# Keys and values of a token tile from one pass over weights that lie side by side, in a linear-attention and MLP kernel

## The chip, the cores and the metric

The kernel runs on one core of a Trainium2 chip. The metric is the device time of one execution, in microseconds (us). Of the kernel before, three runs are given; their median is the time that the change is compared with.

## The reference

Input x has 2048 tokens of D = 640 columns, everything in float32. After a layernorm without weights, xn feeds two branches, and their product is added to x:

```python
xn = _layernorm(x, axis=-1)
q, k, v = (xn @ wqkv) split by thirds, H = 32 heads of Dh = 20
pq = einsum("bhsd,hdf->bhsf", q, w_phi);  pk = einsum("bhsd,hdf->bhsf", k, w_phi)
phi_q = concat([softmax(pq), softmax(-pq)]);  phi_k = concat([softmax(pk), softmax(-pk)])
kv = einsum("bhsf,bhsd->bhfd", phi_k, v);  z = phi_k summed over the tokens
o = (phi_q kv) / (phi_q z + 1e-6);  s = o @ wo
g = silu(gelu(xn @ w1 + b1) @ w2 + b2)
result = x + s * g
```

The hidden width of the second branch is 1536. The change touches only the first part of the first branch: k and v, the features of k, and what they wait for.

## The kernel before, in words

**Arithmetic.** A float32 matrix product is made of products of a reduced type (fp32r in the profile). Each operand is split into an upper part (the value rounded to the type) and a lower part (value minus upper part). `PASSES` lists the three of the four combinations that are computed: upper with upper, upper with lower, lower with upper. The 640 rows of a weight are KC = 5 slices of 128, so one projection of a tile of 128 tokens takes 5 x 3 = 15 steps, and each step has two products (`MATMUL` rows of the profile) of 320 columns, one for each of two PSUM banks.

**Tiles and their order.** The 2048 tokens are 16 tiles of 128 rows. Two tiles make a pair; tile t is half o = t % 2 of pair q = t // 2. The transposed, split x of the pairs stands in `xp` and `beside` (`b` or `b12` in the profile); `stat_x` (L256) picks the 128 x 128 block that a product loads as its stationary operand. Tiles 0 to 7 are loaded as rows (`x_in`, L455), normalised in place and transposed on TensorE (`transpose_x`, L312; its copies out of PSUM are `plain`, L252 on ACT and L254 on DVE). For tiles 8 to 15 the transposed x is loaded from memory instead, and only the statistics are computed from rows: `pair_stats` (L286) runs the statistics on DVE (L197), and for the second tile of a pair it stores mean and factor to memory (L293) and loads them back into all partitions as `bc` (L295). Both are issued by SP, whose instructions run in order, so that a load issued behind L295 goes out only after L295 did.

**Weights.** The weights of queries and keys are multiplied by w_phi ahead of time: `fold` (L168) makes one slice with six small products (L173) into PSUM; `fold_w` (L178) takes its upper part on ACT (L183) and its lower part on DVE (L184). The five slices of the keys, `wk_s`, are made at the start, those of the queries, `wq_s`, between the tiles: slice 0 in tile 3, slice 1 in tile 4, slices 2 and 3 in tile 5, slice 4 in tile 6. The values' weights `wv_s` are loaded and split (`split_w`, L144: upper on ACT, lower on POOL or DVE). Each slice of each weight is one buffer of 2 x 640 columns, upper and lower part.

**PSUM.** `bankA()` hands out one of three buffers of two banks each in turn; `bankB()` hands out one of two single banks, and one of those is held by the accumulators `kv` through the whole stage. The chip's PSUM has no other bank left.

**One tile.** `project(t, ws)` (L323, products at L332) fills a bankA buffer with 30 products of 320 columns. For the keys, `feat1` (L341) reads it on DVE: maximum, minimum (L345, L346), the subtraction (L349), and their difference; then POOL makes the second half (L353). `feat2` (L357) is the exponential on ACT. `key_fin` (L389) sums on DVE, and POOL scales (L371). `value(t)` (L374) is a projection of its own, whose bank ACT copies out (L380) into rows of 21 columns a head. `kv_acc` (L395) multiplies key features and values into `kv` with 32 small products (L403). `query(t)` (L383) projects with `wq_s` and sends the features to memory.

**Order.** In this stage the order of every engine is that of the program text (`manual_schedule`, L462 and L468); each engine works through its instructions in order, and only semaphores between engines make it wait. Tiles 0 and 1 are written out (L499 to L520); a loop runs tiles 2 to 5 (L521 to L541) and another tiles 6 to 15 (L543 to L589). In the first loop the order of a tile is: key projection, `kv_acc` of tile t - 2, key features, in tile 5 the fold of query slice 2, the statistics, then the value projection with the transposes of tile t + 2 in its midst, the exponential, the fold of a query slice, and `key_fin`. Tile 6 has the key projection, `kv_acc` of tile 4, the load of tile 11, statistics of tile 10, features, the fold of query slice 4, value projection, `key_fin`, the first two queries. From tile 7 on, each tile has one or two queries. At the end of tile 15 the first weights of the MLP are brought into their forms (`w1_forms`, L412, with L426 on ACT and L427 on POOL), and the MLP follows in units (products at L650 and L679), with the numerators (L780), the denominators and the output projection (L844) among them.

Of the kernel before, what the change touches and what calls it, by code (L numbers as in the profile page):

```python
# [20 lines left out]
KC = D // P  # L21
HALF = D // 2
# [4 lines left out]
VW = 704  # L27
LN_EPS = 1e-5
DEN_EPS = 1e-6
NH = 2  # L30
SLOTS = 4
FOLD_W = 800
# [14 lines left out]
def hedgehog_gated_mlp_kernel(ctx: ExitStack, tc: tile.TileContext, x, xt_in, wqk, bd, wv, wo, w1, b1, w2, b2, out_t):  # L47
    nc = tc.nc
# [32 lines left out]
    def slab(dt, name, shape=(P, 2, D)):  # L81
        return slabs.tile(list(shape), dt, tag="S", name=name)
# [95 lines left out]
    def fold_w(tl, cs, name, dst):  # L178
        for c in cs:
            ps, mm = fold(tl, c)  # L180
            sl = slab(F32R, f"{name}{c}")
            s3 = sl[:].rearrange("p s (a b) -> p s a b", a=2)
            nc.scalar.activation(s3[:, 0], ps[:, :, :HALF], AF.Copy)  # L183
            lo = nc.vector.tensor_tensor(s3[:, 1], ps[:, :, :HALF], s3[:, 0].bitcast(F32), op=OP.subtract)  # L184
            dst.append(sl)
        return mm, lo


# [123 lines left out]
    def transpose_x(t):  # L312
        q, o = divmod(t, 2)
        xn = xns.pop(t)
        ps = bankA()
        flat = ps[:].rearrange("p a b -> p (a b)")
        for k in range(KC):
            nc.tensor.transpose(flat[:, k * P:(k + 1) * P], xn[:, k * P:(k + 1) * P], ident[:])  # L318
        plain(q, o, flat[:, :D].rearrange("p (k t) -> p k t", t=P))

    PASSES = ((0, 0), (0, 1), (1, 0))

    def project(t, ws, mid=None, at_k=3):  # L323
        q, o = divmod(t, 2)
        ps = bankA()
        n = 0
        for k in range(KC):
            if k == at_k and mid is not None:
                mid()
            for a, b in PASSES:  # L330
                for hf in range(2):
                    nc.tensor.matmul(ps[:, hf, :HALF], stat_x(q, o, k, a),  # L332
                                     ws[k][:, b, hf * HALF:(hf + 1) * HALF],
                                     start=n == 0, stop=n == 3 * KC - 1)
                n += 1
        return ps

    def heads(ps):
        return ps[:, :, :HALF].rearrange("p a (h d) -> p a h d", d=DH)

    def feat1(ps):  # L341
        p4 = heads(ps)
        mx = small.tile([P, 2, 16], F32, tag="mx", name="mx")
        mn = small.tile([P, 2, 16], F32, tag="mn", name="mn")
        nc.vector.tensor_reduce(mx[:], p4, axis=AX.X, op=OP.max)  # L345
        nc.vector.tensor_reduce(mn[:], p4, axis=AX.X, op=OP.min)  # L346
        e = slab(F32, "e")[:]
        e5 = e.rearrange("p a (h s d) -> p a h s d", s=2, d=DH)
        nc.vector.tensor_tensor(e5[:, :, :, 0, :], p4, mx[:, :, :, None].to_broadcast([P, 2, 16, DH]),  # L349
                                op=OP.subtract)  # L350
        nr = small.tile([P, 2, 16], F32, tag="nr", name="nr")
        last_feat[0] = nc.vector.tensor_tensor(nr[:], mn[:], mx[:], op=OP.subtract)  # L352
        nc.gpsimd.tensor_tensor(e5[:, :, :, 1, :], nr[:, :, :, None].to_broadcast([P, 2, 16, DH]),  # L353
                                e5[:, :, :, 0, :], op=OP.subtract)
        return e.rearrange("p a b -> p (a b)")
# [5 lines left out]
    def features(ps):  # L361
        return feat2(feat1(ps))
# [9 lines left out]


    def value(t, mid=None):  # L374
        ps = project(t, wv_s, mid)
        v = row([P, VW], F32, "v")
        v3 = v[:, :32 * (DH + 1)].rearrange("p (h d) -> p h d", d=DH + 1)
        nc.gpsimd.memset(v3[:, :, DH:DH + 1], 1.0)
        nc.gpsimd.memset(v[:, 32 * (DH + 1):], 0.0)
        nc.scalar.activation(v3[:, :, :DH].rearrange("p (a h) d -> p a h d", a=2), heads(ps), AF.Copy)  # L380
        return v

    def query(t):  # L383
        ef = features(project(t, wq_s))
        nc.scalar.dma_start(e_dram[_tok(t)], ef)

    kvp = [None]
# [16 lines left out]
                                         phi[:, 40 * h:40 * h + 40], start=t == 0 and s == 0, stop=t == NT - 1,  # L404
                                         skip_group_check=True)

    vs, es, phis, xns, wk_s, wq_s = {}, {}, {}, {}, [], []

    def load_w1(g):
        return [load_raw(w1[f]) for f in range(g * GF, (g + 1) * GF)]  # L410
# [67 lines left out]
    x_in(7)  # L478
    nc.sync.dma_start(b1t[:], b1)
    nc.sync.dma_start(b2t[:], b2)  # L480
    wv_s = []

    def split_v(c):
        wv_s.append(split_w(wv_raw[c][:], "wv", "dve" if c == 3 else "pool"))

    nc.vector.tensor_tensor(foldb[:120, :, :120].rearrange("p i (k d) -> p i k d", k=6),
                            foldc[:120, :, None, :].to_broadcast([120, 6, 6, DH]),
                            hmask[:120, None, :, None].to_broadcast([120, 6, 6, DH]), op=OP.mult)
    fold_w(wkT, range(1), "wk", wk_s)
    norm_a(0)  # L490
    fold_w(wkT, range(1, 2), "wk", wk_s)
    norm_b(0)
    fold_w(wkT, range(2, 4), "wk", wk_s)
    transpose_x(0)
    norm_a(1)
    fold_w(wkT, range(4, KC), "wk", wk_s)
    norm_act(1)
    norm_a(2)
    split_v(0)  # L499
    kvp[0] = bankB("kv")  # L500
    pk = project(0, wk_s, lambda: transpose_x(1), 4)
    norm_act(2)
    split_v(1)
    split_v(2)
    es[0] = feat1(pk)
    split_v(3)
    pk = project(1, wk_s, lambda: transpose_x(2))
    x_in(8)
    x_in(9)
    load_xr(4)  # L510
# [8 lines left out]
    norm(4)  # L519
    phis[1] = key_fin(es.pop(1))  # L520
    for t in range(2, 6):  # L521
        pk = project(t, wk_s)
        kv_acc(t - 2, phis.pop(t - 2), vs.pop(t - 2))
        es[t] = feat1(pk)
        if t == 5:
            fold_w(wqT, range(2, 3), "wq", wq_s)
        if t < 4:
            norm(t + 3)
        if t == 3:
            norm(7)  # L530
        if t > 3:
            pair_stats(t + 4)
        if t in (3, 4):
            spill(t - 3)
        if t == 5:
            x_in(10)
        vs[t] = value(t, (lambda: transpose_x(t + 2)) if t < 6 else None)
        feat2(es[t])
        if t >= 3:
            fold_w(wqT, range(t - 3 + (t > 4), t - 2 + (t > 4)), "wq", wq_s)  # L540
        phis[t] = key_fin(es.pop(t))  # L541
    queries = iter(range(NT))
    for t in range(6, NT):  # L543
        u = t + 4
        pk = project(t, wk_s)
        if t == 6:
            kv_acc(4, phis.pop(4), vs.pop(4))
        if u < NT:
            if u + 1 < NT:
                x_in(u + 1)  # L550
            pair_stats(u)
            if u % 2:
                load_xr(u // 2)
        if t in (6, 8):
            spill(t // 2 - 1)
        if t % 2 == 0 and 6 < t < NT - 2:
            pair_sub((t + 2) // 2)
        es[t] = feat1(pk)
        if t == 6:
            pair_sub(4)  # L560
            fold_w(wqT, range(4, KC), "wq", wq_s)
        if t % 2 == 0 and t < NT - 2:
            pair_mul((t + 2) // 2)
        if t == 12:
            w1r = load_w1(0)
        if t % 2 and t < NT - 2:
            t_sums((t + 1) // 2)
        vs[t] = value(t)
        feat2(es[t])
        phis[t] = key_fin(es.pop(t))  # L570
        if t % 2 == 0 and 6 < t < NT - 2:
            pair_plain((t + 2) // 2)
        if t % 2 and t < NT - 2:
            t_split((t + 1) // 2)
        if t == 6:
            query(next(queries))
            query(next(queries))
            pair_plain(4)
        if t == NT - 1:
            w1f = w1_forms(w1r)  # L580
            next(w1f)
            next(w1f)
        if t >= 7:
            query(next(queries))
        kv_acc(t - 1, phis.pop(t - 1), vs.pop(t - 1))
        if t == NT - 1:
            next(w1f)
        if 7 <= t < 10:
            query(next(queries))  # L589
    t = NT - 1  # L590
    w2r = [load_raw(w2[f * P:(f + 1) * P, :]) for f in range(GF)]
    pq = project(next(queries), wq_s)
    e_14 = feat1(pq)
    next(w1f)
    w1g = next(w1f)
# [263 lines left out]
        return [load_raw(w2[f * P:(f + 1) * P, :]) for f in range(g * GF, (g + 1) * GF)]  # L859

    kvr = kv_rest()
    e_last = feat1(project(next(queries), wq_s))
    startup.close()
    phase1.close()
    early_psum.close()
# [223 lines left out]
```

## Time and profile before

| | us |
|---|---|
| runs of the kernel before | 682.97, 684.15, 684.3 |
| median | 684.15 |
| span of the profiled execution (first to last instruction) | 681.1 |
| device time of the profiled execution | not given by its page |
| TensorE (PE) | 676.4 busy, 99%, 4727 products |
| weight loads (PEld, beside PE) | 592.0, 87% |
| VectorE (DVE) | 454.8, 67%, 729 instructions |
| GpSimd (POOL) | 382.2, 56%, 351 |
| ScalarE (ACT) | 253.0, 37%, 400 |

Busy shares are means over the span. The granted clock of TensorE is at nine tenths or more in each of the 40 slices of the page. In the rows that follow, a line of the timeline has the start in us from the beginning of the span, the length in us, the engine, the line of the kernel, the operation, output and input with their shapes, the count of instructions that are taken together (x30), and in brackets the engine's idle time in front and what ended it. A line of the chain has the time, the length, the engine, the output and line, and the count. SPq is SP's queue of DMA issues.

### The profile page before, as it was taken

The numbers are of one execution on the slowest core, as the hardware profiler recorded it, in microseconds if no ns is written. First come the engines' busy times: TensorE is split into PE (matmuls) and PEld (weight loads), VectorE is DVE, ScalarE is ACT, GpSimd is POOL, SyncE is SP. The second block draws the span as 40 slices with busy tenths as digits, with TensorE's granted clock in tenths as the row PEclk, the third lists the DMA queues.
The fourth block names the chain that finished last, engine by engine and source line by source line (L and its number), as shares of the span: only waits on it lengthen the run. The fifth ranks groups of instructions, "written<-read, shape, count | busy, mean of one in ns | idle before, by whom it ended". The sixth has DMA issues, their size and how long they took to land.

```text
span 681.1 us, 11991 instructions
## 1 busy us (share of the span) xinstructions
PE 676.4 (99%) x4727; PEld 592.0 (87%) x4727; DVE 454.8 (67%) x729; ACT 253.0 (37%) x400; POOL 382.2 (56%) x351
## 2 busy tenths in 40 slices
PE   9999999999999999999999999999999999999998
PEld 9999999999999998888888888888888887777876
DVE  5786665887876466586978784576876655774232
ACT  3523214333223337144254247533133254425440
POOL 3653254757767375857978952726446640783221
PEclk9999999999999999999999999999999999999999
DMA  8820144633451333329688696476363491888423
GB/s 330 311 80 1 11 142 100 227 93 137 69 200 60 115 138 135 117 88 348 209 273 278 237 426 280 129 259 224 139 216 137 151 398 47 321 296 291 150 94 109
DMA packets 73966, 125.42 MB, mean 184 GB/s; under 512 B 5822, under 2 KB 42686, under 8 KB 73014
## 3 DMA queue, kind: packets, MB, share of 16 engines
q1 hardware_dynamic: 71606, 114.17, 49.3%
q10 hardware_dynamic: 2304, 10.49, 4.4%
q8 instruction: 37, 0.61, 0.4%
q14 instruction: 19, 0.16, 0.1%
HBM read 79.54 MB, written 45.10 MB: 183 GB/s over the span
## 4 chain that ended last, share of the span: by engine, by line
PE 96%; DVE 1%; POOL 1%; issue 1%; ACT 0%; POOLq 0%
PE pA L332 30%; PE pB L679 24%; PE pB L650 22%; PE pB L844 11%; PE pB L780 3%; PE pB L769 2%; PE kv L403 2%; PE pA L173 1%; POOL wv L148 1%; PE pA L466 1%; PE pA L318 1%; PE pB L787 1%; DVE st L197 0%; DVE wk L184 0%; PE pB L624 0%
## 5 line engine op out<-in xcount | busy, mean ns | idle before, releaser
L679 PE MATMUL pB<-hs,w2s 128*128 128x512 f32 x720 | 167.1, 390 | 0.0
L679 PEld LDWEIGHTS pB<-hs,w2s 128*128 128x128 f32 x720 | 134.6, 188 | 29.4 <-PE pB L780 0.8
L650 PE MATMUL pB<-xp,w1s 128*128 128x512 f32 x324 | 81.4, 390 | 0.0
L650 PE MATMUL pB<-xd,w1s 128*128 128x512 f32 x324 | 79.3, 389 | 0.0
L358 ACT ACTIVATE e<-e 128x1280 f32<-128x1280 f32 x32 | 40.7, 1272 | 90.1 <-POOL e L353 89.5
L844 PE MATMUL pB<-oT,wo 128*128 128x512 f32 (+2 forms) x315 | 73.9, 386 | 0.0
L688 DVE TENSOR_TENSOR y<-pB,y 128x512 f32<-128x512 f32 x100 | 63.9, 680 | 12.4 <-PE pB L679 12.2
L650 PEld LDWEIGHTS pB<-xp,w1s 128*128 128x128 f32 x324 | 60.7, 188 | 12.9 <-DVE pB L925 0.4
L650 PEld LDWEIGHTS pB<-xd,w1s 128*128 128x128 f32 x324 | 60.8, 188 | 12.6
L844 PEld LDWEIGHTS pB<-oT,wo 128*128 128x128 f32 x315 | 57.1, 188 | 14.2 <-ACT ph L772 1.2
L371 POOL TENSOR_TENSOR e<-e,rc 128x1280 f32<-128x1280 f32 x16 | 39.0, 2438 | 48.8 <-DVE rc L391 48.4
L371 POOL TENSOR_TENSOR eq<-eq,rc 128x1280 f32<-128x1280 f32 x16 | 37.9, 2369 | 50.2 <-DVE rc L738 50.2
L353 POOL TENSOR_TENSOR e<-nr,e 128x640 f32<-128x640 f32 x32 | 45.5, 1424 | 30.1 <-DVE nr L352 27.7
L332 PE MATMUL pA<-wv,xp 128*128 128x320 f32 x384 | 60.7, 311 | 0.3 <-POOL wv L148 0.3
L655 ACT ACTIVATE pB<-pB,b1t 128x512 f32<-128x512 f32 x48 | 31.8, 662 | 77.2 <-DVE pB L925 27.6
L332 PE MATMUL pA<-wk,xp 128*128 128x320 f32 x384 | 59.9, 311 | 0.0
L332 PE MATMUL pA<-wq,xp 128*128 128x320 f32 x384 | 59.0, 309 | 0.0
L332 PEld LDWEIGHTS pA<-wv,xp 128*128 128x128 f32 x384 | 56.9, 188 | 0.6 <-POOL wv L148 0.5
L332 PEld LDWEIGHTS pA<-wq,xp 128*128 128x128 f32 x384 | 56.9, 188 | 0.1
L332 PEld LDWEIGHTS pA<-wk,xp 128*128 128x128 f32 x384 | 56.8, 188 | 0.1
L725 POOL TENSOR_TENSOR ez<-eq,zrep 128x1280 f32<-128x1280 f32 x16 | 47.3, 2959 | 0.2 <-PE pB L780 0.2
L427 POOL TENSOR_TENSOR w1s<-raw,w1s 128x640 fp32r<-128x640 f32 (+1 forms) x18 | 25.7, 1428 | 36.4 <-ACT w1s L426 29.2
(145 smaller groups left out, 1053.3 us busy)
## 6 DMA issues: line engine op xcount, KB each, us to landing
raw<-in_w_dram SPq DMA_DIRECT2D x42, 320.0 KB, 4.7
e_dram<-e ACTq DMA_DIRECT2D x16, 640.0 KB, 3.8
eq<-e_dram SPq DMA_DIRECT2D x16, 640.0 KB, 6.6
phi_dram<-eq SPq DMA_DIRECT2D x16, 640.0 KB, 3.5
phi<-phi_dram SPq DMA_DIRECT2D x16, 640.0 KB, 9.0
xt<-in_x_dram SPq DMA_DIRECT2D x16, 320.0 KB, 5.7
xres<-in_xt_dram SPq DMA_DIRECT2D x20, 256.0 KB, 4.3
out_dram<-xres SPq DMA_DIRECT2D x18, 256.0 KB, 3.0
```

What stands on the lines that cost most here:

```text
L332: nc.tensor.matmul(ps[:, hf, :HALF], stat_x(q, o, k, a), ws[k][:, b, hf * HALF:(hf + 1) * HALF], start=n == 0, stop=n == 3 * KC - 1)
L353: nc.gpsimd.tensor_tensor(e5[:, :, :, 1, :], nr[:, :, :, None].to_broadcast([P, 2, 16, DH]), e5[:, :, :, 0, :], op=OP.subtract)
L358: nc.scalar.activation(ef, ef, AF.Exp)
L371: nc.gpsimd.tensor_tensor(e3, e3, rc[:, :, None].to_broadcast([P, 64, DH]), op=OP.mult)
L427: nc.gpsimd.tensor_tensor(sl[:, 1, :n], src, sl[:, 0, :n].bitcast(F32), op=OP.subtract)
L650: nc.tensor.matmul(bank[ch][:], tl[:, a, off + wo_:off + wo_ + P], mov(blk, b), start=new and n == 0, stop=n == len(mms) - 1, skip_group_c ...
L655: nc.scalar.activation(ps, ps, AF.Gelu_apprx_tanh, bias=b1t[:, f:f + 1])
L679: nc.tensor.matmul(ps[:], ws[i][:, b, d * P:(d + 1) * P], hs[o][i][:, a, :], start=i == n == 0, stop=(i, n) == (GF - 1, 2), skip_group_che ...
L688: nc.vector.tensor_tensor(y, ps[:], y, op=OP.add)
L725: nc.gpsimd.tensor_tensor(zv, ef, zf, op=OP.mult)
L780: nc.tensor.matmul(po[64 * e:64 * e + 64, :256], bdk[:n, 2 * j + e, :], ph[:n, e * 256:(e + 1) * 256], start=True, stop=True)
L844: nc.tensor.matmul(ps[:, mv], w, o[:, mv], start=n == 0, stop=n == 15, skip_group_check=True)
```

## The change

**Weights.** `wkv` replaces `wk_s` and `wv_s`. For each of the five slices it holds two buffers, one of upper and one of lower parts, and each has 640 columns of keys and, right behind them, 640 of values. `fold_w` writes the key half and `split_v` the value half; their work is the same as before. The number of buffers and their size stay as they were.

**Projection.** For tiles 2 to 15 a new `project_kv` takes the place of the two calls of `project`. The 1280 columns are cut at 512 and at KV1 = 1020. A first pass has 15 steps of two products, columns 0 to 511 and 512 to 1019, into the two banks of one bankA buffer, laid out flat: all 640 key columns and the first 19 heads of the values. A second pass has 15 products of 260 columns, the last 13 heads of the values, into the free bank of bankB. The transposes of tile t + 2, in tiles 2 to 5, stand between the passes. So a tile has 45 products where it had 60, for the same 15 x 1280 columns.

**Readers.** `keys_of` gives the key features the first 640 columns of the flat buffer; they reach 128 columns into the second bank, where the values begin. `values_of` gives the values in two pieces, and `value_row` copies each with an ACT instruction of its own: 19 heads from the second bank of bankA and 13 from bankB.

**Order.** Both passes now stand at the head of a tile, ahead of `kv_acc` in the text, and the value copies stand directly behind the key features: ahead of the fold of query slice 2 in tile 5 and of slice 4 in tile 6, and ahead of the statistics in tiles 2 to 5. Tiles 0 and 1 and all queries keep `project`, with the weight given as a function (`w_part`).

```diff
+KV1 = 1020
...
-            sl = slab(F32R, f"{name}{c}")
-            s3 = sl[:].rearrange("p s (a b) -> p s a b", a=2)
-            nc.scalar.activation(s3[:, 0], ps[:, :, :HALF], AF.Copy)
-            lo = nc.vector.tensor_tensor(s3[:, 1], ps[:, :, :HALF], s3[:, 0].bitcast(F32), op=OP.subtract)
-            dst.append(sl)
+            if dst is wkv:
+                dst.append([slab(F32R, f"{name}{c}{b}") for b in "hl"])
+                s0, s1 = (w[:, 0, :].rearrange("p (a b) -> p a b", a=2) for w in dst[c])
+            else:
+                sl = slab(F32R, f"{name}{c}")
+                s0, s1 = (sl[:, b, :].rearrange("p (a b) -> p a b", a=2) for b in range(2))
+                dst.append(sl)
+            nc.scalar.activation(s0, ps[:, :, :HALF], AF.Copy)
+            lo = nc.vector.tensor_tensor(s1, ps[:, :, :HALF], s0.bitcast(F32), op=OP.subtract)
         return mm, lo
...
+    def w_part(which):
+        if which == "q":
+            return lambda k, b: wq_s[k][:, b, :]
+        return lambda k, b: wkv[k][b][:, "kv".index(which), :]
+
+    def project_kv(t, mid=None):
+        q, o = divmod(t, 2)
+        ps, pv = bankA(), bankB("pv")
+        flat = ps[:].rearrange("p a b -> p (a b)")
+        w = lambda k, b: wkv[k][b][:].rearrange("p a b -> p (a b)")
+        steps = [(k, a, b) for k in range(KC) for a, b in PASSES]
+        for cols in (((0, 512, flat), (512, KV1, flat)), ((KV1, 2 * D, pv[:]),)):
+            for n, (k, a, b) in enumerate(steps):
+                for c0, c1, dst in cols:
+                    d0 = 0 if c0 == KV1 else c0
+                    nc.tensor.matmul(dst[:, d0:d0 + c1 - c0], stat_x(q, o, k, a), w(k, b)[:, c0:c1],
+                                     start=n == 0, stop=n == 3 * KC - 1)
+            if mid is not None:
+                mid()
+                mid = None
+        return flat, pv
...
-                                     ws[k][:, b, hf * HALF:(hf + 1) * HALF],
+                                     ws(k, b)[:, hf * HALF:(hf + 1) * HALF],
                                      start=n == 0, stop=n == 3 * KC - 1)
                 n += 1
-        return ps
+        return heads(ps)
...
-    def feat1(ps):
-        p4 = heads(ps)
+    def feat1(p4):
...
     def value(t, mid=None):
-        ps = project(t, wv_s, mid)
+        return value_row([(project(t, w_part("v"), mid).rearrange("p a h d -> p a (h d)"), 0, H)])
+
+    def value_row(parts):
         v = row([P, VW], F32, "v")
         v3 = v[:, :32 * (DH + 1)].rearrange("p (h d) -> p h d", d=DH + 1)
         nc.gpsimd.memset(v3[:, :, DH:DH + 1], 1.0)
         nc.gpsimd.memset(v[:, 32 * (DH + 1):], 0.0)
-        nc.scalar.activation(v3[:, :, :DH].rearrange("p (a h) d -> p a h d", a=2), heads(ps), AF.Copy)
+        for src, h0, h1 in parts:
+            if len(src.shape) == 3:
+                nc.scalar.activation(v3[:, h0:h1, :DH].rearrange("p (a h) d -> p a h d", a=2),
+                                     src.rearrange("p a (h d) -> p a h d", d=DH), AF.Copy)
+            else:
+                nc.scalar.activation(v3[:, h0:h1, :DH], src.rearrange("p (h d) -> p h d", d=DH), AF.Copy)
         return v
 
+    def keys_of(flat):
+        return flat[:, :D].rearrange("p (a h d) -> p a h d", a=2, d=DH)
+
+    def values_of(flat, pv):
+        h1 = (KV1 - D) // DH
+        return value_row([(flat[:, D:KV1], 0, h1), (pv[:, :2 * D - KV1], h1, H)])
+
     def query(t):
-        ef = features(project(t, wq_s))
+        ef = features(project(t, w_part("q")))
...
     def split_v(c):
-        wv_s.append(split_w(wv_raw[c][:], "wv", "dve" if c == 3 else "pool"))
+        hi, lo = (w[:, 1, :] for w in wkv[c])
+        nc.scalar.activation(hi, wv_raw[c][:], AF.Copy)
+        (nc.vector if c == 3 else nc.gpsimd).tensor_tensor(lo, wv_raw[c][:], hi.bitcast(F32), op=OP.subtract)
...
     for t in range(2, 6):
-        pk = project(t, wk_s)
+        pk = project_kv(t, lambda: transpose_x(t + 2))
         kv_acc(t - 2, phis.pop(t - 2), vs.pop(t - 2))
-        es[t] = feat1(pk)
+        es[t] = feat1(keys_of(pk[0]))
+        vs[t] = values_of(*pk)
         if t == 5:
             fold_w(wqT, range(2, 3), "wq", wq_s)
...
-        vs[t] = value(t, (lambda: transpose_x(t + 2)) if t < 6 else None)
         feat2(es[t])
...
-        pk = project(t, wk_s)
+        pk = project_kv(t)
         if t == 6:
             kv_acc(4, phis.pop(4), vs.pop(4))
...
-        es[t] = feat1(pk)
+        es[t] = feat1(keys_of(pk[0]))
+        vs[t] = values_of(*pk)
         if t == 6:
             pair_sub(4)
             fold_w(wqT, range(4, KC), "wq", wq_s)
...
-        vs[t] = value(t)
         feat2(es[t])
```

More of the change, by code (lines that the diff above doesn't have):

```diff
@@ L405, in kv_acc @@
                                          skip_group_check=True)
-    vs, es, phis, xns, wk_s, wq_s = {}, {}, {}, {}, [], []
+    vs, es, phis, xns, wkv, wq_s = {}, {}, {}, {}, [], []
     def load_w1(g):
@@ L480, in hedgehog_gated_mlp_kernel @@
     nc.sync.dma_start(b2t[:], b2)
-    wv_s = []
     def split_v(c):
-        wv_s.append(split_w(wv_raw[c][:], "wv", "dve" if c == 3 else "pool"))
+        hi, lo = (w[:, 1, :] for w in wkv[c])
+        nc.scalar.activation(hi, wv_raw[c][:], AF.Copy)
+        (nc.vector if c == 3 else nc.gpsimd).tensor_tensor(lo, wv_raw[c][:], hi.bitcast(F32), op=OP.subtract)
     nc.vector.tensor_tensor(foldb[:120, :, :120].rearrange("p i (k d) -> p i k d", k=6),
@@ L488, in hedgehog_gated_mlp_kernel @@
                             hmask[:120, None, :, None].to_broadcast([120, 6, 6, DH]), op=OP.mult)
-    fold_w(wkT, range(1), "wk", wk_s)
+    fold_w(wkT, range(1), "wk", wkv)
     norm_a(0)
-    fold_w(wkT, range(1, 2), "wk", wk_s)
+    fold_w(wkT, range(1, 2), "wk", wkv)
     norm_b(0)
-    fold_w(wkT, range(2, 4), "wk", wk_s)
+    fold_w(wkT, range(2, 4), "wk", wkv)
     transpose_x(0)
     norm_a(1)
-    fold_w(wkT, range(4, KC), "wk", wk_s)
+    fold_w(wkT, range(4, KC), "wk", wkv)
     norm_act(1)
@@ L500, in hedgehog_gated_mlp_kernel @@
     kvp[0] = bankB("kv")
-    pk = project(0, wk_s, lambda: transpose_x(1), 4)
+    pk = project(0, w_part("k"), lambda: transpose_x(1), 4)
     norm_act(2)
@@ L506, in hedgehog_gated_mlp_kernel @@
     split_v(3)
-    pk = project(1, wk_s, lambda: transpose_x(2))
+    pk = project(1, w_part("k"), lambda: transpose_x(2))
     x_in(8)
@@ L591, in hedgehog_gated_mlp_kernel @@
     w2r = [load_raw(w2[f * P:(f + 1) * P, :]) for f in range(GF)]
-    pq = project(next(queries), wq_s)
+    pq = project(next(queries), w_part("q"))
     e_14 = feat1(pq)
@@ L861, in hedgehog_gated_mlp_kernel @@
     kvr = kv_rest()
-    e_last = feat1(project(next(queries), wq_s))
+    e_last = feat1(project(next(queries), w_part("q")))
     startup.close()
```

## The prediction, made before the changed kernel was run

> **What bounds the kernel now.** I read the page first (busy shares, the clock row, the chain that ended last), then the chain in order of time, then the timelines of single engines around the places that the change touches.
>
> ```profile
> span 681.1 us, 11991 instructions
> ...
> PE 676.4 (99%) x4727; PEld 592.0 (87%) x4727; DVE 454.8 (67%) x729; ACT 253.0 (37%) x400; POOL 382.2 (56%) x351
> ...
> PE 96%; DVE 1%; POOL 1%; issue 1%; ACT 0%; POOLq 0%
> ```
>
> TensorE is the bound nearly throughout: 96% of the chain is PE work, so a microsecond taken from PE's stream, or a microsecond for which PE waits, moves the end by that much. The pieces of the chain are dense enough to give PE's pace, as time to the next piece over the count:
>
> ```profile
> 0.84 4.61 PE pA L466 x20
> ...
> 67.18 4.40 PE pA L332 x30
> 71.58 0.77 PE kv L403 x62
> 72.35 1.53 PE pA L173 x12
> ...
> 76.52 0.55 PE pA L318 x5
> 77.07 1.76 PE pA L332 x12
> 78.83 1.33 PE pA L173 x12
> ...
> 291.78 13.60 PE pB L679 x60
> ...
> 560.06 1.45 PE pB L780 x12
> ```
>
> A product of 320 columns takes 4.40 / 30 = 146.7 ns, one of 512 columns 13.60 / 60 = 226.7 ns. The line through both is 0.4167 ns a column and 13.3 ns for each product. So columns cost the same before and after, and the change can only save the 13.3 ns.
>
> **The change, term by term.** Fourteen tiles (2 to 15) use the new routine. A tile had 60 products of 320 columns: 60 x 146.7 = 8.80 us. It gets 15 of 512 (3.40), 15 of 508 at 225.0 (3.38) and 15 of 260 at 0.4167 x 260 + 13.3 = 121.7 (1.83): 8.60 us. The saving is 0.20 a tile, **2.8 us** in all. The 260-column price is not shown by the trace: the nearest rows are the products of L780, 256 columns in 1.45 / 12 = 120.8 ns, and the transposes of L318, which load a full 128 x 128 block each and pass in 0.55 / 5 = 110 ns. 110 bounds the reloading of the array from above, under 121.7, so the load cannot become the limit. With 125 ns instead, the saving would be 2.1 us; with no fixed cost at all, 2.8 stays the most.
>
> The rule of the Trainium skill here is in TensorE: Matmul & The Clock Gate, section Back-to-back issue gap: columns over 2.4 GHz plus about 2.5 ns. By it the 210 removed products would save an estimated 0.5 us. The two rows above disagree with the 2.5 (13.3 ns), so I keep 2.8.
>
> Now the waits. Before, keys were finished 4.40 us after a tile began; now they come with the first pass, after 6.78. In tiles 2 to 5 the five transposes and the copies behind them (lines 252 and 254) are issued ahead of the key features on DVE. And the value copies stand on ACT directly behind the features, ahead of the query folds (line 183) at tiles 5 and 6; before, those folds came first. The place where this meets a deadline is tile 6. The rows of before:
>
> ```profile
> 73.92 0.71 ACT L183 ACTIVATE wq<-pA 128x640 fp32r<-128x640 f32 x1 [5.58 <-PE pA L173]
> 77.10 0.38 ACT L252 ACTIVATE b<-pA 128x256 fp32r<-128x256 f32 x1 [2.48 <-PE pA L318]
> 77.38 0.49 ACT L252 ACTIVATE xp<-pA 128x384 fp32r<-128x384 f32 x1
> 86.90 0.70 ACT L183 ACTIVATE wq<-pA 128x640 fp32r<-128x640 f32 x1 [5.52 <-PE pA L173]
> 91.36 0.71 ACT L380 ACTIVATE v<-pA 128x640 f32<-128x640 f32 x1 [3.76 <-PE pA L332]
> ```
>
> ```profile
> 74.66 0.82 DVE L184 TENSOR_TENSOR wq<-pA,wq 128x640 fp32r<-128x640 f32 x1 [0.65 <-ACT wq L183]
> 77.90 0.42 DVE L254 TENSOR_TENSOR b<-pA,b 128x256 fp32r<-128x256 f32 x1 [1.14 <-ACT xp L252]
> 78.25 0.55 DVE L254 TENSOR_TENSOR xp<-pA,xp 128x384 fp32r<-128x384 f32 x1
> 87.14 0.89 DVE L197 BATCH_NORM_STATS2 st<-xt 128x6 f32<-128x320 f32 x2 [2.93 <-DMA xt<-in_x_dram]
> 88.44 0.81 DVE L345 TENSOR_REDUCE mx<-pA 128x32 f32<-128x640 f32 x1
> 89.90 0.81 DVE L349 TENSOR_TENSOR e<-pA,mx 128x640 f32<-128x640 f32 x1
> 90.73 0.82 DVE L184 TENSOR_TENSOR wq<-pA,wq 128x640 fp32r<-128x640 f32 x1
> ```
>
> ```profile
> 77.36 0.36 SPq L293 DMA_DIRECT2D st_dram<-pst  x1
> 80.79 0.33 SPq L295 DMA_DIRECT2D bc<-st_dram  x1
> 81.22 0.86 SPq L141 DMA_DIRECT2D xt<-in_x_dram  x2
> ```
>
> ```profile
> 91.10 4.56 PE L332 MATMUL pA<-wq,xp 128*128 128x320 f32 x30
> ```
>
> The reader is to see a chain that no PE row shows. After the fold of slice 2 (DVE at 74.66) come tile 9's statistics; their store starts at 77.36; SP waits for it to land before the broadcast load at 80.79, and tile 10's rows are asked for only behind that, at 81.22. They land at 87.14, and DVE stands idle for them 2.93 us, with tile 6's features queued behind (88.44) and the fold of slice 4 behind those (90.73, done at 91.55). Query 0 starts at 91.10 and meets slice 4 with its 25th product, 24 x 0.1467 = 3.52 us later, at 94.6: three microseconds to spare. From 74.66 to 88.44 it is 13.78 us, set by transfers and not by PE; I carry it over.
>
> The same in the new order, from zero at the end of tile 5's first pass. **PE:** transposes 0.55, second pass 1.83, accumulation 0.77, folds 1.53 and 1.33, tile 6's passes 6.78 and 1.83, accumulation 0.77, fold 1.53, 24 products of query 0 3.52: slice 4 is wanted at 20.44. **The chain:** ACT takes the transposes at 0.58 (77.10 against their end at 77.07); DVE's first copy follows 0.80 later (77.10 to 77.90) at 1.38, its second ends at 2.28, the features begin at 2.2 and their last read of the bank ends 2.27 later (88.44 to 89.90 + 0.81) at 4.47. Then ACT copies the values: 380 columns at 0.49 and 260 at 0.38, by the rows of 384 and 256 columns at 77.38 and 77.10, overlapping by about 0.1 as those do; the fold's ACT half starts at 5.16, its DVE half 0.74 later (73.92 to 74.66) at 5.90. Plus 13.78: tile 6's features at 19.68, bank read until 21.95, value copies, slice 4 on ACT 22.66 to 23.36 and on DVE 23.40 to 24.22. PE wants the upper part at 20.44 and gets it at 23.39: 2.95 us. After two products (0.29) it wants the lower part and gets it at 24.25: 0.57. **A wait of 3.5 us**, where there was none. Behind it on PE stand query 1 and all later tiles. What queues behind the blocked value copy on ACT is just this fold.
>
> That ACT must wait for DVE's reads is read off the row at 77.90. DVE's copy of b needs only ACT's copy of b, done at 77.48; it starts at 77.90, when ACT's copy of xp, out of the same bank, ends at 77.87. The keys' last 128 columns and the first 380 of the values share a bank, so I take it that the two engines' reads are ordered there too.
>
> The Trainium skill states this as a rule, in PSUM — Partial Sum Buffer, section PSUM bank collisions raise a hardware error: two engines may not touch one bank at once, "ScalarE-read with VectorE-read included", and compilers order them. The trace agrees by the row at 77.90.
>
> One more small wait, at the end of the stage, from these rows:
>
> ```profile
> 236.39 0.70 ACT L380 ACTIVATE v<-pA 128x640 f32<-128x640 f32 x1 [4.65 <-PE pA L332]
> 238.29 1.49 DVE L366 TENSOR_REDUCE rc<-e 128x64 f32<-128x1280 f32 x1 [3.91 <-ACT e L358]
> 240.51 2.36 POOL L371 TENSOR_TENSOR e<-e,rc 128x1280 f32<-128x1280 f32 x1 [4.65 <-DVE rc L391]
> 250.96 1.29 POOL L427 TENSOR_TENSOR w1s<-st,w1s 128x512 fp32r<-128x512 f32 x1 [2.42 <-ACT w1s L426]
> 252.71 1.52 PE L650 MATMUL pB<-xd,w1s 128*128 128x512 f32 x6
> ```
>
> Tile 15's keys come 2.4 us later, its value copy no longer holds up the exponential, and the scaling on POOL (240.51) starts about 1.15 later against the tile's start, with the MLP's weight forms behind it on POOL. Their lower part ends at 252.25; PE wants it with the third product from 252.71, about 253.2, which now comes 0.2 sooner: 0.95 of cover against 1.35. I take **0.3 us**, between 0 and 1.0.
>
> What is covered: the second value copy frees its one bank about 5.3 us after the first pass, and the next second pass writes it no sooner than 0.55 + 1.83 + 0.77 + 6.78 = 9.9. The extra ACT copy is 0.17 a tile on an engine that is 37% busy. The accumulators wait for key features that come 2.4 us later; in tiles 7 and on they have a query and a whole tile, over 13 us, to hide it. Bank buffers become fewer by one a tile, which eases PE.
>
> **Sum:** -2.8 + 3.5 + 0.3 = +1.0 us. It is made against the profiled execution, whose page gives a span of 681.1 and no device time of its own; the timed runs (682.97 to 684.3) lie 1.9 to 3.2 above that span. Carried to the median of 684.15: **685.2 us**, with its own range of 684.4 to 686.4, from the term at the end (0 to 1.0) and an estimated 0.5 us either way in the landing of tile 10's rows.
>
> **Rivals.**
> 1. *The clock falls in the wait* (slower side). The first 20 products, 128 columns of plain fp32, take 4.61 / 20 = 230 ns, the transposes of the same shape at 76.52 0.55 / 5 = 110 ns: PE began at half pace and lost 2.4 us. If a PE idle for most of 3.5 us falls back to that pace and climbs as slowly, 2.4 us come on top: 687.6. It decides from the point where the idle stretch is long enough; no wait of before is longer than 0.8, so the trace can neither bear it out nor exclude it. The page on TensorE (same one, section Why this matters for your kernels) has the rule that gaps above about 3 us drop the clock; mine is 2.95 by this sum, at its edge.
> 2. *More waits than found*: another late landing or a bank chosen worse, 1.5 to 2 us: 687.
> 3. *Reads of a bank are not ordered between ACT and DVE.* Then slice 2 is folded 0.45 sooner and slice 4's ACT half is early; only the DVE half at 21.5 to 22.3 is late: 1.65 us. Sum -1.15: 683.0. The row at 77.90 speaks against it.
> 4. *No wait at all*, because tile 10's rows land earlier. The full saving: 681.3. They would have to land 3.5 us sooner; the row of the page for this load says how late they were here:
>
> ```profile
> xt<-in_x_dram SPq DMA_DIRECT2D x16, 320.0 KB, 5.7
> ```
>
> The sixteen loads take 5.7 us in the median, this one 87.14 - 81.22 = 5.92: only 0.2 of the 3.5 is bad luck.
>
> **Chances.** Forecast 0.48, rivals 0.15, 0.10, 0.12, 0.15. What a measurement of this kernel can tell from no change is 0.2%, 1.4 us: below 682.8 is faster, above 685.5 slower. Of the forecast 0.30 is same and 0.18 slower; rival 3 is 0.09 same and 0.03 faster. Slower 0.43, same 0.39, faster 0.18. The range 682.4 to 688.0 leaves out rival 4 and the ends of 1 and 2.
>
> **What will show it.** Right: 512- and 508-column products at about 226 ns and 260 at 122; a PE wait at line 332 for ACT's and DVE's fold (lines 183 and 184) near 92 us, about 3.5 in two pieces; the value copy starting only when the feature subtraction ends. Wrong: that copy starting at the first pass's end (rival 3), tile 10's statistics not DVE's longest wait near 90 us (rival 4), PE rows of twice their length after the wait (rival 1), or PE waits for anything else (rival 2).

## The result, and the profile after

The changed kernel takes **690.38 us** (median of four runs, 690.13 to 690.78) against 684.08 (four runs, 682.97 to 684.3): **6.3 us slower**, ratio 1.010 with an interval of 1.0087 to 1.0112. 685.2 was forecast, with 688.0 as the upper end. The direction of the likeliest case was right; the size was short by more than 5 us.

The page of the changed kernel, the lines that answer to those of before:

```profile
span 689.1 us, 11585 instructions
...
PE 678.7 (98%) x4517; PEld 575.6 (84%) x4517; DVE 448.6 (65%) x729; ACT 254.3 (37%) x414; POOL 380.8 (55%) x351
...
PE 89%; DMA 4%; DVE 3%; POOL 1%; issue 1%; ACT 1%; SPq 0%; DVEq 0%; POOLq 0%
```

210 products are gone (4517 against 4727), and yet PE was busy 2.3 us longer. So there are two losses to look for: time in which PE waits, and time in which it works more slowly. The waits of PE, in us in total, times and longest:

```profile
PE pA L359 <- ACT wq L189: 2.6, 1, 2.6
PE pB L690 <- DVE e L375: 2.5, 1, 2.5
PE pA L506 <- PEq L1119: 0.8, 1, 0.8
PE pA L359 <- DVE wq L190: 0.3, 1, 0.3
...
PE pB L820 <- DVE oT L824: 0.3, 1, 0.3
```

The first and the fourth are the predicted wait in query 0 (L332, L183 and L184 of before are L359, L189 and L190 now). The second, as long, was in no part of the prediction: the first product of the MLP (L690, before L650) waits for the subtraction in the features of the last query. The third was there before.

The slower work is in the stretches behind those two waits. Each row has the start and end of a stretch, its length, the busy time of PE, PEld, DVE, ACT and POOL in it (in brackets their instructions), PE's granted clock, the DMA share and GB/s:

```profile
94.00:96.90 2.90, 0.29 (x2) 0.02 (x1) 1.51 (x4) 1.36 (x3) 1.25 (x2) 1.00 0.91 297
96.90:98.30 1.40, 1.09 (x5) 0.83 (x6) 0.82 (x1) 1.27 (x1) 1.40 (x4) 1.00 0.04 15
98.30:101.70 3.40, 3.40 (x15) 3.40 (x14) 1.70 (x2) 0.00 (x0) 1.67 (x1) 0.50 0.00 0
```

```profile
255.00:257.50 2.50, 0.03 (x2) 0.04 (x1) 2.44 (x4) 2.02 (x6) 1.54 (x2) 1.00 0.63 262
257.50:258.70 1.20, 1.20 (x5) 1.00 (x6) 1.00 (x1) 0.00 (x0) 1.20 (x2) 1.00 0.00 0
258.70:262.10 3.40, 3.40 (x10) 2.61 (x9) 0.00 (x0) 2.35 (x3) 3.22 (x5) 0.51 0.14 41
```

PE resumes at full clock, and 1.3 to 1.4 us later the clock falls to 0.50 for 3.41 us, after both waits. Half of 3.41 is lost each time: 1.7 us. The page's clock row, in tenths over slices of 17 us, shows 9 throughout and hides it.

Last, the pace of the new products, from the chain:

```profile
123.98 6.92 PE pA L343 x30
130.90 1.78 PE pv L343 x15
132.68 4.39 PE pA L359 x30
```

A first pass takes 6.92 us, not 6.78; a second pass 1.78, not 1.83. A tile costs 8.70 against 8.80.

**The sum of the two profiles.** From the first product of tile 2 to the end of the last query, PE took 218.1 us before (33.4 to 251.5) and takes 221.6 now (33.4 to 255.0). Without the wait of 2.62 + 0.30 and the 1.7 of half clock behind it, 217.0 are left: the merged products save **1.1 us**, where 2.8 were predicted. So -1.1 + 2.9 + 1.7 (query 0) + 2.5 + 1.7 (MLP) + 0.3 (the last line of the waits) = +8.0, and the spans differ by 689.1 - 681.1 = 8.0. The medians differ by less, 6.3: the profiled execution of before is at the low end of that kernel's runs (in a later series of 21 its spans were 680.9 to 682.6), and that of after has the longest span of its four (688.4 to 689.1).

### The profile page after: what moved, and what is told of

Read it like the earlier page. It is cut to its first block, busy times and chain, and to the rows that moved or that the text cites. A ratio compares the mean times of both kernels' runs of the same rounds, so it can differ in the third digit from the quotient of the medians.

```text
span 689.1 us, 11585 instructions
## 1 busy us (share of the span) xinstructions
PE 678.7 (98%) x4517; PEld 575.6 (84%) x4517; DVE 448.6 (65%) x729; ACT 254.3 (37%) x414; POOL 380.8 (55%) x351
## 4 chain that ended last, share of the span: by engine, by line
PE 89%; DMA 4%; DVE 3%; POOL 1%; issue 1%; ACT 1%; SPq 0%; DVEq 0%; POOLq 0%
PE pB L719 22%; PE pB L690 20%; PE pA L343 13%; PE pB L884 11%; PE pA L359 11%; PE pv L343 3%; PE pB L820 3%; DMA raw<-in_wo_dram 2%; PE pB L809 2%; PE kv L443 2%; DMA phi<-phi_dram 1%; DMA xt<-in_x_dram 1%; PE pA L174 1%; PE pA L506 1%; DVE st L202 1%
## 5 line engine op out<-in xcount | busy, mean ns | idle before, releaser
L690 PE MATMUL pB<-xp,w1s 128*128 128x512 f32 x324 | 81.8, 391 | 2.5 <-DVE e L375 2.5
L690 PE MATMUL pB<-xd,w1s 128*128 128x512 f32 x324 | 80.5, 393 | 0.0
L690 PEld LDWEIGHTS pB<-xp,w1s 128*128 128x128 f32 x324 | 61.1, 189 | 15.5 <-ACT kvr L643 2.7
L690 PEld LDWEIGHTS pB<-xd,w1s 128*128 128x128 f32 x324 | 61.6, 190 | 12.9
L359 PE MATMUL pA<-wq,xp 128*128 128x320 f32 x384 | 59.7, 310 | 2.9 <-ACT wq L189 2.6
L359 PEld LDWEIGHTS pA<-wq,xp 128*128 128x128 f32 x384 | 56.8, 188 | 3.5 <-ACT wq L189 2.9
L812 ACT ACTIVATE ph<-pB 120x512 f32<-120x512 f32 (+1 forms) x48 | 23.9, 561 | 43.7 <-PE pB L809 29.9
L392 DVE TENSOR_REDUCE rc<-e 128x64 f32<-128x1280 f32 x16 | 23.7, 1483 | 24.0 <-ACT e L384 23.9
L371 DVE TENSOR_REDUCE mx<-pA 128x32 f32<-128x640 f32 x32 | 25.8, 805 | 20.8 <-PE pA L343 15.1
L706 ACT ACTIVATE x<-pB 128x512 f32<-128x512 f32 x12 | 7.2, 599 | 80.8 <-PE pB L690 80.8
```

The costliest lines, as they stand in the source:

```text
L359: nc.tensor.matmul(ps[:, hf, :HALF], stat_x(q, o, k, a), ws(k, b)[:, hf * HALF:(hf + 1) * HALF], start=n == 0, stop=n == 3 * KC - 1)
L690: nc.tensor.matmul(bank[ch][:], tl[:, a, off + wo_:off + wo_ + P], mov(blk, b), start=new and n == 0, stop=n == len(mms) - 1, skip_group_c ...
```

## The experiments

All are timed beside the kernel before on the same chip; a ratio is to that kernel (683.1 to 683.4 us in these series), with its interval. In the series of the change the kernel before took 684.08, so times that were worked out from 690.4 stand 0.7 to 0.9 us too high for these series; the differences to the kernel before are the better measure. An idle product is one whose result nobody reads.

### The layout alone

The weights as in the change, but every tile projects keys and values apart, in the old order:

```diff
-        pk = project_kv(t)
+        pk = project(t, w_part("k"))
...
-        es[t] = feat1(keys_of(pk[0]))
-        vs[t] = values_of(*pk)
+        es[t] = feat1(pk)
...
+        vs[t] = value(t)
         feat2(es[t])
```

> The changed kernel's weights (keys and values of a slice side by side, upper and lower parts in buffers of their own), but every tile projects keys and values apart, with four products of 320 columns a step, in the order of the kernel before. Theory: the layout costs nothing, the products, banks and waits are those of before: 683.2 to 683.4, ratio 0.999 to 1.001. Rival (the operand read out of the wider buffers is slower, or the buffers take each other's place): over 684.5, with a spacing of the 320-column products over 147 ns.

Measured: 683.08, ratio 1.0001 (0.9992 to 1.001). The chain has 90 products in 13.40 us and 120 in 17.80, as before. The layout costs nothing; all that follows comes of the merged products and the order that they bring.

### The wait in query 0: where it starts

The early load: tile 10's rows are loaded ahead of tile 9's store and broadcast load on SP.

```diff
+        if t == 5:
+            x_in(10)
         if t > 3:
             pair_stats(t + 4)
...
-        if t == 5:
-            x_in(10)
```

> The changed kernel with the load of tile 10's rows issued on SP ahead of tile 9's statistics store and its broadcast load, and nothing else moved. Theory (the prediction's chain): the rows land some 3 us sooner, DVE no longer stands idle for them, the features of tile 6 start when their bank is full (86.5 us), and the fold of slice 4 is done before query 0 wants it: the wait and the half clock behind it go as in the early fold, 690.4 - 4.6 = 685.8, or 684.7 by the run of the early fold. Rival (the features or the value copies are late for another reason than the landing): the wait shrinks by less than 1.5 us and the time stays over 688.

Measured: 685.38, ratio 1.0033 (1.002 to 1.0046). In the changed kernel, SP issues the load at 85.71 behind the broadcast load, and DVE's statistics wait for it (SP first, then DVE):

```profile
85.28 0.33 SPq L300 DMA_DIRECT2D bc<-st_dram  x1
85.71 0.86 SPq L142 DMA_DIRECT2D xt<-in_x_dram  x2
```

```profile
79.70 0.82 DVE L190 TENSOR_TENSOR wq<-pA,wq 128x640 fp32r<-128x640 f32 x1 [1.33 <-ACT wq L189]
...
91.83 0.89 DVE L202 BATCH_NORM_STATS2 st<-xt 128x6 f32<-128x320 f32 x2 [7.31 <-DMA xt<-in_x_dram]
...
96.89 0.82 DVE L190 TENSOR_TENSOR wq<-pA,wq 128x640 fp32r<-128x640 f32 x1 [1.39 <-ACT wq L189]
```

DVE of the experiment:

```profile
84.39 0.82 DVE L202 BATCH_NORM_STATS2 st<-xt 128x6 f32<-128x320 f32 x2
...
86.68 0.82 DVE L371 TENSOR_REDUCE mx<-pA 128x32 f32<-128x640 f32 x1 [0.97 <-PE pA L343]
```

Statistics at 84.39 and not 91.83, features as soon as PE has filled their bank, and no wait in query 0. The one DMA that stood behind another on SP was the cause; the rival is out. The eight runs lie between 683.74 and 687.82: the wait at the MLP is still there, and whether the clock falls behind it differs (below). The highest of the eight is more than that explains: its mean clock is 0.995, as in the changed kernel with its two stretches at half clock, but it has no trace, and its cause stays open.

### The same wait, cut at the fold

The early fold: slice 4 is folded right behind the accumulation, ahead of tile 10's statistics.

```diff
             kv_acc(4, phis.pop(4), vs.pop(4))
+            fold_w(wqT, range(4, KC), "wq", wq_s)
...
             pair_sub(4)
-            fold_w(wqT, range(4, KC), "wq", wq_s)
```

> The changed kernel with one thing moved: in tile 6 the fold of query slice 4 is issued right behind the accumulation of tile 4, ahead of tile 10's statistics, so that neither half of it stands behind the late features or the value copies. Theory: the wait of 2.62 + 0.30 us in query 0 goes, and with it the 3.41 us at half clock that follow it (1.7 us): 690.4 - 4.6 = 685.8, one half-clock stretch left, at the start of the MLP. Rival (the half clock at 98 us has another cause than the wait): only 2.9 go, 687.5, and two half-clock stretches stay. Rival (another late instruction stands right behind): under 1 us goes, over 689.4.

Measured: 684.72, ratio 1.0023 (1.0013 to 1.0033), 5.0 us better against the kernel before than the change is. The wait in query 0 is gone:

```profile
PE pB L690 <- DVE e L375: 2.5, 1, 2.5
PE pA L174 <- DMA folds<-in_wqk_dram: 1.3, 1, 1.3
```

(The second is at the start, where the first weights land now sooner, now later.) One half-clock stretch is left in the profiled run. Of the ten runs, the four with a mean clock of 0.996 or 0.997 take 685.64 to 686.73, the six with 0.999 or 1.000 take 683.89 to 684.89: 1.9 us apart in the mean, about what one half-clock stretch costs. (Only one of the ten, at 686.73, has a trace.)

### Only ACT's order

The value copies of tile 6 behind the fold:

```diff
         es[t] = feat1(keys_of(pk[0]))
-        vs[t] = values_of(*pk)
         if t == 6:
             pair_sub(4)
             fold_w(wqT, range(4, KC), "wq", wq_s)
+        vs[t] = values_of(*pk)
```

> The changed kernel with the value copies of tile 6 issued behind the fold of slice 4 instead of ahead of it; DVE's order is as in the change. Theory: ACT's half is then early and only DVE's half behind the features is late (from 94.6 to about 96.3): one wait of about 1.7 us in place of 2.62 + 0.30, so 1.2 less: 689.2; and if a wait of 1.7 us leaves the clock alone, 1.7 less again: 687.5. Which of the two, and whether it is the same in every run, shows how long a wait the clock stands. Rival (the value copies are not what holds ACT's half): 690.4.

Measured: 687.5, ratio 1.0063 (1.0049 to 1.0077). ACT, and PE below it:

```profile
90.86 0.71 ACT L189 ACTIVATE wq<-pA 128x640 fp32r<-128x640 f32 x1 [9.24 <-PE pA L174]
95.85 0.49 ACT L413 ACTIVATE v<-pA 128x380 f32<-128x380 f32 x1 [4.28 <-DVE e L375]
```

```profile
96.70 0.85 PE L359 MATMUL pA<-wq,xp 128*128 128x320 f32 x4 [2.12 <-DVE wq L190]
97.39 1.92 PE L359 MATMUL pA<-wq,b 128*128 128x320 f32 x12
```

ACT's half of the fold is early, so it was the value copies that held it, and they wait for DVE's last read of the shared bank. DVE's half alone still costs 2.12 us, where 1.7 was worked out. The twelve products of the next query take 1.92; in the changed kernel, with the half clock on them, they take 3.36:

```profile
98.56 3.36 PE L359 MATMUL pA<-wq,b 128*128 128x320 f32 x12
```

So a wait of 2.12 us went by without a half clock here. That the median is the 687.5 that was worked out is partly luck: against the kernel before it is 2.0 us better than the change, where 2.9 stood, and in the profiled run (686.72) the wait at the MLP passes without a half clock as well.

### The wait at the MLP: which bank the last query lies in

The kernel before, with one idle product into a bankA buffer ahead of its last query, and nothing else:

```diff
+    nc.tensor.matmul(bankA()[:, 0, :P], one, one, start=True, stop=True)
     e_last = feat1(project(next(queries), wq_s))
```

> The kernel before with the same idle product ahead of its last query: there it moves the last query into the bank that the MLP's first product writes. Nothing else of the change is in it. Theory: a wait of 2.5 us (features read their bank until 2.49 us after the MLP's first product could start) and 1.7 us of half clock appear: 684.1 + 4.2 = 688.3. Rival (the wait comes of the new projection, not of which buffer is the last): 684.2.

Measured: 687.32, ratio 1.0053 (1.0039 to 1.0067): 3.9 us. The kernel before as it is (first PE, then DVE), and then with the idle product:

```profile
251.32 1.55 PE L650 MATMUL pB<-xp,w1s 128*128 128x512 f32 x6
```

```profile
253.00 0.81 DVE L349 TENSOR_TENSOR e<-pA,mx 128x640 f32<-128x640 f32 x1
```

```profile
254.16 2.88 PE L650 MATMUL pB<-xp,w1s 128*128 128x512 f32 x6 [2.47 <-DVE e L349]
```

DVE reads the last query's bank until 253.81 in the kernel before, 2.5 us after the MLP's first product. That was free because the last query lay in another buffer than the one whose bank the MLP writes first. The three buffers go round; with one more handed out the last query comes to lie in that one, and the 2.47 us appear, followed by 3.41 us at half clock. The change takes one buffer fewer in each of 14 tiles, and in a turn of three 14 fewer is the same as one more. Nothing else of it is needed for this wait. (The numbers of the banks are not in the trace.)

The other way round, in the changed kernel:

```diff
+    nc.tensor.matmul(bankA()[:, 0, :P], one, one, start=True, stop=True)
     e_last = feat1(project(next(queries), w_part("q")))
```

> The changed kernel with one idle product of 128 columns into a bankA buffer ahead of the last query, so that this query goes to other banks than the one that the first product of the MLP writes. Theory: the wait of 2.47 us for the last features' reads goes, and the half clock behind it (1.7 us), less 0.1 to 0.2 for the added product: 690.4 - 4.1 = 686.3. Rival (the MLP's first product waits for the features for another reason than the shared bank): 690.4 or a little more.

Measured: 688.31, ratio 1.0068 (1.0054 to 1.0081). Less than the 4.1 us expected: against the kernel before it is 1.4 us better than the change by the medians, about 2.2 by the ratios, 3.0 by the profiled spans. The waits say a part of why:

```profile
PE pA L359 <- ACT wq L189: 2.6, 1, 2.6
PE pA L506 <- PEq L1120: 0.8, 1, 0.8
PE pB L690 <- ACT kvr L643: 0.7, 1, 0.7
```

The wait for the features is gone, but the seventh product of the MLP waits 0.7 us for the copies out of `kv`, which the longer wait had covered. The idle product takes 0.25 us. So the trace shows 2.5 + 1.7 - 0.7 - 0.25 = 3.2 us gained, near the 3.0 of the spans; what the medians lack of that, up to 1.8 us, isn't assigned.

### Both

The early fold and the idle product together.

> Both edits: the early fold and the idle product. Theory: both waits and both half-clock stretches go, 690.4 - 4.6 - 4.1 = 681.7, and what is left against the kernel before is the saving of the merged products: by the product spacings (6.91 + 1.78 against 8.80 us a tile) 14 x 0.11 = 1.5 us, so 682 to 683, ratio 0.997 to 0.998. Rival (the merged products save nothing, the profile of before was a lucky run): 684.0, ratio 1.000. By the prediction's 2.8 us: 681.3.

Measured: 683.15, ratio 0.9995 (0.9986 to 1.0004); eleven runs within 0.33 us, with a clock of 0.999 or 1.000 in all. The two edits take back the whole 6.3 us. They leave no gain that shows, where 682 to 683 was expected. In this run's trace the products save 1.4 us from tile 2 to the last query (216.9 with the 0.25 of the idle product, against 218.1); with +0.7 for the copies of `kv`, +0.25 for the idle product and +0.3 late in the kernel that comes to -0.15, and -0.2 was measured.

### The width of the second product

As both, and the second product of a step 512 columns wide; the last four are computed here and again in the second pass:

```diff
-        for cols in (((0, 512, flat), (512, KV1, flat)), ((KV1, 2 * D, pv[:]),)):
+        for cols in (((0, 512, flat), (512, 1024, flat)), ((KV1, 2 * D, pv[:]),)):
```

> Both edits (early fold, idle product) and the second product of a step widened from 508 to 512 columns; the four added columns are computed twice, and nobody reads the first result. Measured spacing in the first pass is 230.3 ns a product where 225.8 was predicted. Theory (the uneven 508 columns cost the 4.5 ns): spacing 226.7, 210 x 2 x 3.6 ns = 1.5 us less: 683.15 - 1.5 = 681.6. Rival (the spacing has nothing to do with the width): 4 columns x 0.4167 ns x 210 = 0.35 us more, 683.5.

Measured: 682.3, ratio 0.9985 (0.9976 to 0.9994).

```profile
155.62 6.83 PE pA L343 x30
162.44 1.78 PE pv L343 x15
```

A pass is 0.09 us shorter although it computes 60 columns more. In the traces the starts of the 508 and 512 mix are 222 to 239 ns apart in a pattern of eight, 230.4 in the mean; with 512 alone most are 226 or 227 apart. Why isn't shown. By these pieces of the chain a tile takes 8.61 us, 0.19 less than before, as the prediction had it: 2.7 us for 14 tiles. Less than that arrives: 0.85 us were gained over the two edits where 1.5 stood, and from tile 2 to the last query the trace has 2.3 us saved, not 2.7.

### The bank of the accumulators

As both, and an idle product into `kv` at the start, so that it is given the bank that it had in the kernel before:

```diff
     kvp[0] = bankB("kv")
+    nc.tensor.matmul(kvp[0][:, :P], one, one, start=True, stop=True)
```

> Both edits, and one idle product of 128 columns into the accumulators' bank at the start, so that this bank is taken before the first pv and the accumulators lie where they lay in the kernel before. Theory (the 0.7 us for which the MLP's seventh product waits for the copies out of the accumulators comes of the accumulators having moved to the bank that the MLP writes second): the wait goes, 683.15 - 0.7 + 0.1 = 682.5. Rival (the copies are late wherever the accumulators lie): 683.2.

Measured: 682.77, ratio 0.9989 (0.998 to 0.9998). The wait for the copies of `kv` goes, and two smaller ones come up behind it:

```profile
PE pB L691 <- DVE pB L967: 0.6, 1, 0.6
...
PE pB L691 <- POOL w1s L467: 0.2, 1, 0.2
```

So the accumulators' bank was the cause of that wait, but the two new ones come to 0.8, as long as the old. By the medians 0.4 is gained, by the differences to the kernel before 0.2; the intervals don't tell it from nothing. The second line is the wait for the MLP's weight forms that the prediction priced at 0.3.

### All four

> The early fold, the idle product ahead of the last query, the accumulators held in their old bank, and the second product of a step at 512 columns. Theory: the gains add up, 683.15 - 0.4 (bank of the accumulators) - 0.85 (512 columns) against a kernel before of 683.2 to 683.4: 681.9, ratio 0.997 to 0.998. Rival (the accumulators' bank and the width gain the same microsecond): 682.4, ratio 0.9985 to 0.999.

Measured: **681.69, ratio 0.998 (0.9971 to 0.9989)**, 1.4 us faster than the kernel before, and so 7.7 us better than the change as it was made, by the differences to the kernel before. No wait of 0.4 us or more is left after the start:

```profile
PE pA L506 <- PEq L1121: 0.8, 1, 0.8
PE pA L359 <- POOL wk4l L524: 0.3, 1, 0.3
PE pA L323 <- DVE xt L218: 0.2, 1, 0.2
PE pB L691 <- POOL w1s L467: 0.2, 1, 0.2
```

The terms, -2.7 + 0.25 + 0.2 (the idle product into `kv` falls into the waits of the start), would give 2.2; the interval reaches to 2.0. In the profiled runs the stretch from tile 2 to the last query is 2.1 us shorter than before, idle product included, and the MLP with what follows is 0.4 longer.

## Why the prediction was wrong

- **The wait in query 0: right, by its mechanism and its size.** The DVE half of slice 2's fold was worked out to start 5.90 us after tile 5's first pass; that pass ends at 73.81 and the fold starts at 79.70. From there to tile 6's features 13.78 was carried over and 13.43 (79.70 to 93.13) measured. The wait is 2.62 + 0.30 where 2.95 + 0.57 stood. Early load, early fold and ACT's order each act as the chain says. Rivals 3 and 4 are out; for rival 3, ACT's copy of the values and DVE's subtraction out of the same bank in tile 5:

```profile
78.31 0.49 ACT L413 ACTIVATE v<-pA 128x380 f32<-128x380 f32 x1 [3.15 <-DVE e L375]
```

```profile
77.46 0.81 DVE L375 TENSOR_TENSOR e<-pA,mx 128x640 f32<-128x640 f32 x1
```

  The copy starts 0.04 us after the subtraction ends.
- **The bank buffers: wrong, and this is the step that failed.** The prediction said: "Bank buffers become fewer by one a tile, which eases PE." It counted buffers and didn't ask which one comes last. The last query moved into the MLP's first bank: 2.5 us of wait and 1.7 of half clock behind it, which the kernel before shows too with one idle product. The numbers to see it were there: DVE reads that query until 253.81, and the MLP starts at 251.32, in a pool that is opened anew over the same banks. Rival 2 named a worse bank in passing, at 1.5 to 2 us and a chance of 0.10, without a place.
- **The clock: rival 1 came true, twice,** and it was given 0.15. Its price was 2.4 us and is 1.7 each time. It was also tied to the one wait that was known; with a second wait it counted double.
- **The saving: mis-sized, 1.1 us for 2.8** (1.4 to 1.5 in the three runs without a wait in query 0 and with the same products: early load, early fold, both). The line through 320 and 512 columns holds for 512 (226.7) and is near for 260 (118.7 for 121.7), but not for 508 columns beside 512. With 512 the passes save 2.7 by their spacing, 2.3 in all. The working also said that with no fixed cost for the 260 columns 2.8 stays the most; by its own line 15 x 13.3 ns a tile would come on top, 5.6 us. Nothing hung on it.
- **The 0.3 us at the MLP's weight forms** doesn't appear in the changed kernel, where the longer wait covers it; 0.2 us of it shows once that wait and the one for the copies of `kv` are gone.

So the terms are -1.1 where -2.8 stood, 2.9 for 3.5, 0 for 0.3, and 1.7 + 2.5 + 1.7 + 0.3 for nothing. What causes the last 0.3, the wait at L820, isn't shown.

## What to carry to other kernels

When a change takes or frees a buffer in a loop, follow the rotation to the end of the loop: which buffer is the last, who reads it and until when, and who writes that memory next, also across the border of a pool. When a wait of two microseconds or more on TensorE is forecast, price it with and without a stretch at half clock behind it, and make that part of the forecast rather than a rival. A merged product that saves a fixed cost of nanoseconds is worth making only with the waits of its new order removed.

## What the runs showed of the hardware

**The clock falls in whole windows of a fixed grid.** In the clock records of the changed kernel's trace, full clock starts at 6.17 us, half clock at 98.33 and again at 258.76: 27 and 74 times 3.413 us after the first. Each stretch at half clock is 3.413 us long. So it looks as if PE's idleness is judged by windows of 3.413 us, and a window with too much of it makes the next one slow. Eight waits of six runs bear this out and show how much. The idle time in the fullest window of each, by the product ends of the trace, which are modelled:

| run | wait | idle in its fullest window | half clock behind it |
|---|---|---|---|
| ACT's order | query 0 | 1.49 | no |
| early load | MLP | 1.80 | no |
| ACT's order | MLP | 1.81 | no |
| change | MLP | 2.14 | yes |
| change | query 0 | 2.29 | yes |
| early fold | MLP | 2.47 | yes |
| idle product in the kernel before | MLP | 2.47 | yes |
| idle product in the change | query 0 | 2.58 | yes |

By these the limit lies between 1.81 and 2.14 of 3.41 us. The same wait of 2.47 us at the MLP costs 1.7 us more or not, by where the grid, whose place differs from run to run, cuts it. In the changed kernel 2.14 of it lie in one window; for the early load a border at 251.79 leaves 1.80 and 0.67, and the clock stays full:

```profile
249.80:252.50 2.70, 0.23 (x3) 0.07 (x1) 2.47 (x4) 2.04 (x7) 1.57 (x2) 1.00 0.58 243
252.50:256.00 3.50, 3.50 (x16) 2.87 (x17) 0.97 (x1) 1.76 (x2) 3.40 (x5) 1.00 0.01 2
```

The Trainium skill has the grid in TensorE: Matmul & The Clock Gate, section What's actually happening: a free-running window of 3413 ns whose activity sets the clock of what follows. The traces agree. Its rule, in the section HAM oscillation — how this bites in real kernels, is that there should be no idle gaps above about 3.4 us; here 2.47 us were enough in three of the five profiled runs that have this wait, and the measurement decides.

**A product of 508 columns between products of 512 is no cheaper than one of 512,** and the pair takes 460.7 ns (2 x 230.4) where two of 512 take 453 (2 x 226.7).
